# Turning blocks of rows every four steps, and a longer planned time for the addition with maximum

## The chip, the cores and the metric

The kernel runs on one core of one Trainium2 chip. The metric is the device time of one execution in microseconds (us); of several runs the median counts. The core has a matrix engine (TensorE, PE in the profile, with its weight loads as PEld), a vector engine (VectorE, DVE), an activation engine (ScalarE, ACT), a general engine (GpSimd, POOL), and a sync engine (SyncE, SP) that here only issues transfers. Each engine and each queue works through its own instructions in the order in which they were written.

## The reference

Two attention branches on the same input are mixed by a gate per row (x is 2048 rows of 512, 32 heads of 16).

```python
def _A_ref(x, wqkv, wo):          # sliding window: 8 keys, two rows apart
    ...
    idx = pos[:, None] - off[None, :]
    kg = k[:, :, idx_c, :] ; vg = v[:, :, idx_c, :]
    logits = einsum("bhsd,bhswd->bhsw", q, kg) * scale     # masked where idx < 0
    o = einsum("bhsw,bhswd->bhsd", softmax(logits), vg)
    return o.transpose(...).reshape(B, S, D) @ wo
def _B_ref(x, wq, wk, wv, wo):    # full attention, one key and value head for 32 query heads
    ...
    p = softmax(einsum("bhqd,bkd->bhqk", q, k) * scale)
    return einsum("bhqk,bkd->bhqd", p, v).transpose(...).reshape(B, S, D) @ wo
g = sigmoid((x * gate_w).sum(-1))
return g * a + (1 - g) * b
```

## The kernel before

The whole schedule is written out by one Python program, with its own clocks for PE, ACT, DVE and POOL (`clk`, `pool`). These clocks decide the order in which instructions are written, no more; on the chip semaphores decide when they run.

**First phase.** Projections of x. Their matmuls fill half of PE's rows each, and two halves side by side make a slot.

**The main loop** has 512 steps: 32 units of branch B (a block of 512 query rows by four heads), each over 16 blocks of 128 keys. In a step PE makes two pairs of score matmuls into banks `pe` (L582), ACT takes two exponentials (L584), and PE weights the values of the step before into `po` (L592). Branch B also needs the maximum of each row's scores ahead of a unit. It comes from extra score matmuls, 2048 tiles over the whole kernel, in three ways:

- a pair into both halves of bank `pm` (L393, from `fill_pair`), whose maximum DVE takes in one instruction (L422): at most one in a step;
- a single into bank `ps` (L393, from `fill_one`), reduced by L433: in the steps where `singles` allows it;
- halves (L491): from one matmul against a difference of keys ACT takes the absolute value (L520), and from one against their sum DVE adds it and takes the maximum in one instruction, with a short read of the accumulator behind it (L537, in `fill_sum`). This is done in the first phase and in the two **out phases**. Two L491 make two tiles, and each lies beside a half of the product that the phase is there for.

**The out phases** (`out_phase`) interrupt the main loop, at step 272 for rows 0 to 7 of each block of 16 and at step 416 for rows 8 to 11; they multiply the finished rows by the output weights (L889, 24 slots a row). The last four rows are done by `spread` inside the steps, from about step 481 on (L943, two or three pairs a step), once the maxima have all been taken. `fill_sum` writes a sum's matmul when the plan says that its bank (`ps` or `po`) is free, that is when the planned DVE clock has passed the sum before; `T_TTR = 0.66` us is what the plan counts for that.

**Branch A** is computed on POOL alongside (L656 to L716), in two halves of the rows, `hf` 0 and 1; `done` holds what POOL's plan has finished. A finished block of rows has to be turned before the out phase: `blocks_out` transposes a 128x256 piece on DVE (L778) into a buffer `raw` or `own`, a transfer writes it to `td` in memory (L783), and eight transfers bring it back (L791). All nine stand in SP's queue, which also loads queries (`qst<-qd`, L362 and L363) and half of the maxima (`qst<-ml`, L570). For each half there is one buffer of each kind; the four pieces queued when `hf` 1 ends (rows 8 to 11, second half of columns) all use `own`, so the transposition of one has to wait until the write of the one before has read it. `block_some(s)` runs at the end of every step and writes one transposition when its time has come.

Of the kernel before, what the change touches and what calls it, by code (L numbers as in the profile page):

```python
# [50 lines left out]
T_R, T_LAT, T_EXP, T_RED2, T_RED1, T_W, T_TTR = 0.23, 0.20, 0.92, 1.14, 0.61, 1.21, 0.66  # L51
# [30 lines left out]
def gated_mix_kernel(ctx, tc, xt, wa, wk, wq, wo_a, wo_b, out):  # L82
# [38 lines left out]
    clk = {"pe": 0.0, "act": 0.0, "dve": 0.0}  # L121

    def after(eng, ready, dur):
        clk[eng] = max(clk[eng], ready) + dur
        return clk[eng]
# [246 lines left out]
    free = {"m2": 0.0, "m1": 0.0, "e0": 0.0, "e1": 0.0, "po": 0.0}  # L372
    tasks, shifted, pm = [], set(), []
    hooks, pool, done = [], 0.0, set()
# [4 lines left out]
    def unit_tile(v):  # L379
        for x in (v, v + 1):  # L380
            if x < NU and x not in left:
                mx[x] = wp.tile([P, 2, 2, 4, 4], F32, name="mx", bufs=3)
                if pe:
                    nc.gpsimd.memset(mx[x], -FMAX)
                    charge(250)
                else:
                    nc.scalar.activation(mx[x].rearrange("p b i t k -> p (b i t k)"), ident[:, 0:64], AF.Identity, scale=0.0, bias=mk[:, 6:7])
                left[x] = NF // NU
        return mx[v]
# [8 lines left out]
    def filled(v, n):  # L398
        left[v] -= n
        if not left[v]:  # L400
            ms = wp.tile([P, 2, 2, 8], F32, name="ms")
            m = mx.pop(v).rearrange("p b i t k -> p b (i t) k")
            nc.vector.tensor_reduce(ms, m.unsqueeze(2).to_broadcast([P, 2, 2, 8, 4]), AX.X, ALU.max)
            after("dve", 0, 0.32)
            if pe:
                tasks.append((clk["pe"] + 0.5, maxima_turn, (v, ms)))
            else:
                maxima_turn(v, ms)
# [80 lines left out]
    def half_mm(dst, v, pr, t, kc, x, odd):  # L489
        b = 64 * odd  # L490
        nc.tensor.matmul(dst, qst[home(v)[0]][b:b + 62, pr, t * P:(t + 1) * P], kcd[0][b:b + 62, kc // 2, x, :], start=True, stop=True)  # L491
# [40 lines left out]
    def fill_sum(odd):  # L532
        (v, pr, t, kc), d, ready = pend[odd].pop(0)
        m = unit_tile(v)
        dst, key = ((m1, "m1"), (po, "po"))[odd]
        half_mm(dst, v, pr, t, kc, 0, odd)
        nc.vector.tensor_tensor_reduce(d[:, odd], dst, d[:, odd], 1.0, -FMAX, ALU.add, ALU.max, m[:, odd, pr, t, kc:kc + 1])  # L537
        free[key] = after("dve", max(clk["pe"] + T_R + T_LAT, ready), T_TTR) + 0.08
        filled(v, 2)

    def shift_a(v, mt):
# [33 lines left out]
    pe, pexp, exped = [], {}, {}  # L575
# [199 lines left out]
    def blocks_out(j, k):  # L775

        own = p2[0].tile([P, D // 2], F32, name="raw", tag=("raw", "own")[k if j < NJ - 4 else 0], bufs=1)
        nc.vector.transpose(own, oa[k][:, j, :])  # L778
        after("dve", clk["pe"], 0.45)
        tasks.append((clk["dve"] + 0.3, blocks_away, (j, k, own)))  # L780
# [13 lines left out]
    block_queue, turned_in, block_at = [], [], [0]  # L794

    def block_some(s):

        for hf in range(2):
            if hf in done and ("blocks", hf) not in done:
                done.add(("blocks", hf))  # L800
                block_queue.extend((j, k) for j in ((0, 1, 2, 3, 4, 5, 6, 7), (8, 9, 10, 11))[hf] for k in range(2) if (hf, k) != (1, 0))
        if 8 in done and ("blocks", 2) not in done:
            done.add(("blocks", 2))
            block_queue.extend((j, 0) for j in range(8, 12))
        if block_queue and s >= block_at[0]:
            blocks_out(*block_queue.pop(0))
            block_at[0] = s + (1 if 1 in done else 4)

    def blocks_both(j):
        blocks_out(j, 0)  # L810
# [29 lines left out]
    def stream(seq, mm, done, pooled, meet=None):  # L840
# [3 lines left out]
        while min(at) < len(seq):  # L844
# [4 lines left out]
            if halves or 1 in wants:  # L849
                for b in range(2):  # L850
                    if sum_ready(b):
                        lone[b] = lambda b=b: fill_sum(b)
                    elif diff_ready(b):
                        lone[b] = lambda b=b: fill_diff(b)
                        break
            elif fillable() and free["m1"] <= clk["pe"] - just():
                lone[half[0][4] if half else 0] = lambda: fill_one(m1, "m1")
            elif pooled and fillable() and free["po"] <= clk["pe"] - just():
                lone[half[0][4] if half else 0] = lambda: fill_one(po, "po")
# [17 lines left out]
    def out_phase(js, n, whole_unit):  # L877
# [34 lines left out]
        while groups or any(pend):  # L912
            for b in range(2):
                if sum_ready(b):
                    fill_sum(b)
                elif diff_ready(b):
                    fill_diff(b)
            clk["pe"] += T_R
# [351 lines left out]
    for s in range(NS + 1):  # L1270
# [65 lines left out]
        run_tasks()  # L1336
        run_pool()
        block_some(s)
    while later_rows:
        clk["pe"] = max(clk["pe"], spread_at[0])  # L1340
# [77 lines left out]
```

## Time and profile before

| what | value |
|---|---|
| runs shown | 1451.13, 1451.15, 1453.5 us; median 1451.15 |
| profiled execution | 1452.75 us, its span 1450.9 us |
| PE, DVE, ACT, POOL busy | 99%, 82%, 88%, 70% of the span |
| transfers | 65 GB/s over the span |
| granted TensorE clock | 0.998 |

The span is the time from the first to the last instruction; the profiled execution's own time is 1.85 us more. In the profile's rows a timeline entry is start, duration, engine, line, operation, result and operands; a bracket gives the idle time before it and what ended it.

### The profile page before, as it was taken

The page shows a single profiled execution, that of the slowest core. Times are in us where ns is not written, and L with a number is a line of the kernel's source. Part 1 is how long each engine was busy: PE and PEld are TensorE (multiplying, and loading weights), DVE is VectorE, ACT ScalarE, POOL GpSimd, SP SyncE. Part 2 cuts the span into 40 slices and gives each one's busy share as a digit, 9 for nine tenths or more (in the row PEclk, how much of TensorE's full clock was granted, in tenths as well). Part 3 has the DMA queues.
Part 4 walks back from the last instruction along what each step waited for, and adds up shares of the span by engine and source line. Part 5 has one row for each costly group of instructions (what it writes and reads, how often), then busy time and mean ns, then how long its engine had stood idle before and what let it go on. Part 6 is the DMA issues. An engine that isn't in the chain of part 4 may idle for free.

```text
span 1450.9 us, 29246 instructions
## 1 busy us (share of the span) xinstructions
PE 1440.6 (99%) x10524; PEld 672.2 (46%) x10524; DVE 1193.9 (82%) x1885; ACT 1280.9 (88%) x1608; POOL 1019.7 (70%) x1796
## 2 busy tenths in 40 slices
PE   9999999999999999999999999999999999999998
PEld 6977777433333333333333475333333336333343
DVE  8978889688888888888888898888888888888712
ACT  6659888999999999999999888999999888999986
POOL 7952989869898888888988987988888615111121
PEclk9999999999999999999999999999999999999999
DMA  7753433222021120212422200211211111000110
GB/s 238 221 157 103 125 104 98 66 55 87 14 84 42 46 90 13 72 42 75 113 72 64 75 31 31 90 54 42 72 43 42 27 26 35 9 2 2 30 30 30
DMA packets 107457, 96.12 MB, mean 66 GB/s; under 512 B 84976, under 2 KB 89120, under 8 KB 103088
## 3 DMA queue, kind: packets, MB, share of 16 engines
q1 hardware_dynamic: 100224, 55.04, 14.0%
q0 software_dynamic: 6368, 37.90, 7.7%
q8 instruction: 83, 1.36, 0.4%
q10 hardware_dynamic: 720, 1.31, 0.3%
q14 instruction: 62, 0.51, 0.1%
HBM read 63.18 MB, written 30.49 MB: 65 GB/s over the span
## 4 chain that ended last, share of the span: by engine, by line
PE 94%; POOL 2%; DVE 2%; DMA 1%; ACT 0%; issue 0%; SPq 0%; ACTq 0%; DVEq 0%
PE po L592 33%; PE pe L582 23%; PE pe L1217 12%; PE pm L393 8%; PE ps L393 6%; PE pe L889 4%; PE pm L491 3%; PE ps L491 2%; PE po L491 1%; PE pm L943 1%; POOL oa L716 1%; POOL av L713 1%; PE pe L227 1%; DMA wqr<-wq 0%; DVE pexp L537 0%
## 5 line engine op out<-in xcount | busy, mean ns | idle before, releaser
L584 ACT ACTIVATE pexp<-pe 128x1024 f32<-128x1024 f32 x1022 | 987.0, 1022 | 85.7 <-PE pe L582 81.5
L422 DVE TENSOR_REDUCE mx<-pm 128x2 f32<-128x1024 f32 x501 | 612.4, 1222 | 136.0 <-PE pm L393 131.7
L592 PE MATMUL po<-pexp,vst 128*32 128x512 f32 x4096 | 546.3, 605 | 0.0
L582 PE MATMUL pe<-qst,kst 64*128 64x512 f32 x1916 | 444.9, 452 | 0.6 <-ACT pexp L584 0.6
L582 PEld LDWEIGHTS pe<-qst,kst 64*128 64x128 f32 x1916 | 180.9, 183 | 474.1 <-ACT pexp L584 467.8
L433 DVE TENSOR_REDUCE mx<-ps 128x1 f32<-128x512 f32 x403 | 274.1, 680 | 3.7 <-PE ps L393 3.7
L393 PE MATMUL pm<-kst,qst 62*128 62x512 f32 x967 | 197.0, 398 | 3.2 <-DVE mx L422 3.2
L656 POOL TENSOR_TENSOR pr<-aext 128x256 f32<-128x256 f32 x256 | 182.1, 738 | 3.0 <-DMA aext<-ad 2.7
L716 POOL TENSOR_TENSOR oa<-oa,av 128x256 f32<-128x256 f32 x224 | 163.9, 732 | 15.5
L592 PEld LDWEIGHTS po<-pexp,vst 128*32 128x32 f32 x4096 | 80.8, 108 | 165.5 <-issue 156.1
L393 PE MATMUL ps<-kst,qst 62*128 62x512 f32 x395 | 156.2, 396 | 0.2 <-DVE mx L537 0.2
L713 POOL TENSOR_TENSOR av<-aext,lg 128x256 f32<-128x256 f32 x224 | 139.2, 622 | 12.9
L520 ACT ACTIVATE dd<-pm 128x512 f32<-128x512 f32 x180 | 101.4, 606 | 16.4 <-PE pm L491 11.2
L1217 PE MATMUL pe<-wah,xl 64*128 64x512 f32 x376 | 109.8, 393 | 0.0
L1217 PE MATMUL pe<-wal,xh 64*128 64x512 f32 x376 | 108.3, 394 | 0.0
L1217 PE MATMUL pe<-wah,xh 64*128 64x512 f32 x376 | 107.2, 395 | 0.4 <-DVE stage L324 0.3
L393 PEld LDWEIGHTS pm<-kst,qst 62*128 62x128 f32 x967 | 94.5, 187 | 7.2 <-DVE mx L422 5.0
L520 ACT ACTIVATE pexp<-pm 128x512 f32<-128x512 f32 x128 | 72.1, 599 | 15.7 <-PE pm L491 7.2
L662 POOL TENSOR_TENSOR tr<-pr 128x512 f32<-128x512 f32 x64 | 81.7, 1277 | 4.2
L662 POOL TENSOR_TENSOR tr<-tr 128x256 f32<-128x256 f32 (+1 forms) x128 | 72.5, 566 | 8.6
L393 PEld LDWEIGHTS ps<-kst,qst 62*128 62x128 f32 x395 | 73.9, 187 | 4.8 <-issue 1.2
L537 DVE CUSTOM_DVE_ANT_0 dd<-po,dd 128x512 f32<-128x512 f32 x90 | 62.1, 690 | 12.4 <-PE po L491 6.7
(222 smaller groups left out, 1942.7 us busy)
## 6 DMA issues: line engine op xcount, KB each, us to landing
aext<-ad POOLq DMA_DIRECT2D x32, 1056.0 KB, 5.6
qst<-qd SPq DMA_DIRECT2D x60, 128.0 KB
ad<-stage SPq DMA_DIRECT2D x32, 240.0 KB
qd<-qhi SPq DMA_DIRECT2D x16, 256.0 KB
qd<-qlo SPq DMA_DIRECT2D x16, 256.0 KB
td<-raw SPq DMA_DIRECT2D x32, 128.0 KB
oa<-td SPq DMA_DIRECT2D x256, 16.0 KB
xraw<-xt SPq DMA_DIRECT2D x15, 256.0 KB
```

Source lines behind the costliest of these rows:

```text
L393: nc.tensor.matmul(dst, qst[home(v)[0]][b:b + 62, pr, t * P:(t + 1) * P], kst[b:b + 62, kc * 512:(kc + 1) * 512], start=True, stop=True)
L422: nc.vector.tensor_reduce(m[:, :, pr, t, kc], dst, AX.X, ALU.max)
L433: nc.vector.tensor_reduce(m[:, odd, pr, t, kc:kc + 1], dst, AX.X, ALU.max)
L520: nc.scalar.activation(d[:, odd], m2[:, odd, :], AF.Abs)
L582: nc.tensor.matmul(bank[:, odd, :], kst[b:b + 64, kt * P:(kt + 1) * P], qst[home(u)[0]][b:b + 64, pr, :], start=True, stop=True)
L584: nc.scalar.activation(e, bank, AF.Exp, scale=SCALE)
L592: nc.tensor.matmul(po[32 * i:32 * i + 32, :], vst[:, kt, :], pexp[s, i // 2][:, i % 2, :], start=(kt == 0), stop=(kt == NJ - 1))
L656: nc.gpsimd.tensor_mul(pr[:, k], q, e[:, o:o + NH, AC:2 * AC])
L662: nc.gpsimd.tensor_add(nx, cur[:, :, 0:n], cur[:, :, n:2 * n])
L713: nc.gpsimd.tensor_mul(av, e[:, o:o + NH, 2 * AC:].rearrange("p j (h d) -> p j h d", d=DH), lg[:, w].unsqueeze(3).to_broadcast([P, NH, AG, ...
L716: nc.gpsimd.tensor_add(ao, ao, av)
L1217: nc.tensor.matmul(front[2 if x == last else x % 2][0][:, b, :], l[h], r[h], start=(i == 0), stop=(i == 3 * C - 1))
```

## The change

```diff
@@ fill_sum
-        free[key] = after("dve", max(clk["pe"] + T_R + T_LAT, ready), T_TTR) + 0.08
+        free[key] = after("dve", max(clk["pe"] + T_R + T_LAT, ready), 0.70 if pe else T_TTR) + 0.08
@@ block_some
         for hf in range(2):
             if hf in done and ("blocks", hf) not in done:
                 done.add(("blocks", hf))
+                block_at[0] = s + 2
                 block_queue.extend(...)
...
-            block_at[0] = s + (1 if 1 in done else 4)
+            block_at[0] = s + 4
```

The added line makes every line number behind it one larger. `pe` is empty in the first phase, so there 0.66 stays. Before, the blocks that follow the first half of branch A already stood four steps apart; those that follow the second half stood one step apart. Now all stand four apart, and the first of a half comes two steps after that half's end.

The counts of what PE does change in one kind of work only: 256 halves (L491) inside the out phases become 232 (168 to 156 in the first, 88 to 76 in the second), and their 24 tiles are made by 13 more matmuls into `pm` and 11 more into `ps`. The sum of matmuls is the same. Up to the first block of rows nothing moves.

**DVE where branch A ends.** First before: the transpositions (`raw<-oa`, the program's name for either buffer) stand one step apart (at the ends of steps 393 to 396), with a pair's and mostly a single's maximum between.

```order
L422 TENSOR_REDUCE mx<-pm 128x2
L778 STREAM_TRANSPOSE raw<-oa_3729 128x256
L422 TENSOR_REDUCE mx<-pm 128x2
L433 TENSOR_REDUCE mx<-ps 128x1
L778 STREAM_TRANSPOSE raw<-oa_3729 128x256
L422 TENSOR_REDUCE mx<-pm 128x2
L433 TENSOR_REDUCE mx<-ps 128x1
L778 STREAM_TRANSPOSE raw<-oa_3729 128x256
```

DVE at the same place now (ends of steps 398 and 402, then 406 and 410):

```order
L778 STREAM_TRANSPOSE raw<-oa_3729 128x256
L422 TENSOR_REDUCE mx<-pm 128x2
L433 TENSOR_REDUCE mx<-ps 128x1
L606 STREAM_TRANSPOSE tt<-po 128x512
L422 TENSOR_REDUCE mx<-pm 128x2
L433 TENSOR_REDUCE mx<-ps 128x1
L613 RECIPROCAL rl<-tt 128x16
L422 TENSOR_REDUCE mx<-pm 128x2 x2
L433 TENSOR_REDUCE mx<-ps 128x1
L778 STREAM_TRANSPOSE raw<-oa_3729 128x256
```

Four steps' maxima now stand between two transpositions. SP's queue there before:

```order
L783 DMA td<-raw 128x256 x2
L791 DMA oa_3729<-td 32x4x32 x8
L783 DMA td<-raw 128x256
L791 DMA oa_3729<-td 32x4x32 x8
L783 DMA td<-raw 128x256
L791 DMA oa_3729<-td 32x4x32 x8
L362 DMA qst_81<-qd 32x1x1024
```

SP's queue there now:

```order
L362 DMA qst_81<-qd 32x1x1024
L363 DMA qst_81<-qd 16x1024
L362 DMA qst_81<-qd 32x1x1024
L363 DMA qst_81<-qd 16x1024
L783 DMA td<-raw 128x256
L570 DMA qst_77<-ml 2x8x32 x4
L791 DMA oa_3729<-td 32x4x32 x8
L783 DMA td<-raw 128x256
```

The load of a unit's queries now goes ahead of the first write to `td`, and four transfers of maxima stand behind it.

**PE at the first out phase's start.** Before:

```order
L889 MATMUL pe_85<-wol_3733,own_10067 128x512
L889 MATMUL pe_85<-woh_3732,own_10068 128x512 x4
L491 MATMUL pm<-q_76,qst_81 128x512
L889 MATMUL pe_85<-woh_3732,own_10068 128x512
L491 MATMUL pm<-q_76,qst_81 128x512
L889 MATMUL pe_85<-woh_3732,own_10068 128x512
L889 MATMUL pe_85<-woh_3730,turned_10071 128x512
```

PE there now (the out product is L890):

```order
L393 MATMUL ps<-kst,qst_81 128x512
L890 MATMUL pe_85<-wol_3733,own_10075 128x512 x5
L890 MATMUL pe_85<-woh_3732,own_10076 128x512 x4
L393 MATMUL pm<-kst,qst_81 128x512 x2
L890 MATMUL pe_85<-woh_3732,own_10076 128x512 x4
L890 MATMUL pe_85<-woh_3730,turned_10079 128x512 x8
L890 MATMUL pe_85<-wol_3731,turned_10079 128x512 x4
L491 MATMUL pm<-q_76,qst_82 128x512
```

The halves start later, and one single and one pair are made in the phase in place of some of them.

**PE where the maxima end and the last rows begin.** Before:

```order
L393 MATMUL pm<-kst,qst_82 128x512
L582 MATMUL pe_86<-qst_81,kst 128x512 x2
L592 MATMUL po<-pexp,vst 32x512 x4
L582 MATMUL pe_85<-qst_81,kst 128x512 x2
L943 MATMUL pm<-woh_3730,turned_15910 128x512 x6
```

PE there now:

```order
L393 MATMUL pm<-kst,qst_82 128x512 x2
L582 MATMUL pe_86<-qst_81,kst 128x512 x2
L592 MATMUL po<-pexp,vst 32x512 x4
L582 MATMUL pe_85<-qst_81,kst 128x512 x2
L393 MATMUL pm<-kst,qst_82 128x512 x2
L582 MATMUL pe_86<-qst_81,kst 128x512 x2
L592 MATMUL po<-pexp,vst 32x512 x4
L582 MATMUL pe_85<-qst_81,kst 128x512 x2
L944 MATMUL pm<-woh_3730,turned_15928 128x512 x6
```

Two more steps take a pair of maxima, the last rows' products begin two steps later, and six later steps (493 to 498) then hold three pairs of those products where they held two.

## The prediction

> **What bounds the kernel.** I read the page's head and chain first, then single steps in the timeline, then the steps that are longer than their kind.
>
> ```profile
> span 1450.9 us, 29246 instructions
> PE 1440.6 (99%) x10524; PEld 672.2 (46%) x10524; DVE 1193.9 (82%) x1885; ACT 1280.9 (88%) x1608; POOL 1019.7 (70%) x1796
> PE 94%; POOL 2%; DVE 2%; DMA 1%; ACT 0%; issue 0%; SPq 0%; ACTq 0%; DVEq 0%
> ...
> 707.79 0.50 PE L582 MATMUL pe<-qst,kst 64*128 64x512 f32 x2
> 709.69 0.49 PE L582 MATMUL pe<-qst,kst 64*128 64x512 f32 x2
> 710.25 0.40 PE L393 MATMUL ps<-kst,qst 62*128 62x512 f32 x1
> 711.81 0.50 PE L582 MATMUL pe<-qst,kst 64*128 64x512 f32 x2
> ...
> 728.16 0.50 PE L582 MATMUL pe<-qst,kst 64*128 64x512 f32 x2
> 730.29 0.49 PE L582 MATMUL pe<-qst,kst 64*128 64x512 f32 x2
> ```
>
> PE is busy for 99% and carries 94% of the chain, so time is won where PE's row is shorter or where it waits. The first L582 of a step marks its start. A step with a pair of maxima takes 1.90 us (707.79 to 709.69), one that also holds a single 2.12 (709.69 to 711.81): a single costs 0.22 and makes one tile. The step at 728.16 holds a single and no pair, and takes 2.13 all the same: a pair put there is free.
>
> The long steps stand together where branch A ends:
>
> ```profile
> 1150.27 0.73 POOL L716 TENSOR_TENSOR oa<-oa,av 128x256 f32<-128x256 f32 x1
> 1151.03 0.45 DVE L778 STREAM_TRANSPOSE raw<-oa 128x256 f32<-128x256 f32 x1 [1.73 <-POOL oa L716]
> 1151.33 0.51 PE L582 MATMUL pe<-qst,kst 64*128 64x512 f32 x2
> 1152.64 0.50 PE L393 MATMUL pm<-kst,qst 62*128 62x512 f32 x2 [0.81 <-DVE mx L422]
> 1155.58 0.45 DVE L778 STREAM_TRANSPOSE raw<-oa 128x256 f32<-128x256 f32 x1
> 1158.03 0.38 SPq L783 DMA_DIRECT2D td<-raw  x1
> 1158.84 0.49 PE L582 MATMUL pe<-qst,kst 64*128 64x512 f32 x2
> 1159.89 0.45 DVE L778 STREAM_TRANSPOSE raw<-oa 128x256 f32<-128x256 f32 x1 [2.16 <-DMA td<-raw]
> 1161.50 0.50 PE L393 MATMUL pm<-kst,qst 62*128 62x512 f32 x2 [2.17 <-DVE mx L422]
> 1163.82 0.79 PE L582 MATMUL pe<-qst,kst 64*128 64x512 f32 x2
> 1171.60 0.49 PE L582 MATMUL pe<-qst,kst 64*128 64x512 f32 x2
> ...
> 1158.00:1162.00 4.00, 1.83 (x14) 0.64 (x8) 2.04 (x4) 2.46 (x3) 0.00 (x0) 1.00 0.30 63
> 1162.00:1167.00 5.00, 5.00 (x27) 1.54 (x24) 3.66 (x5) 2.96 (x3) 3.07 (x7) 0.66 0.28 56
> ```
>
> The first transposition stood 1.73 in DVE until POOL's last sum of branch A, the fourth 2.16 until the third's write, issued 2.4 after it, had left the buffer. The maxima queue behind them on DVE, and PE waits for the bank: 0.81 and 2.17. (The windows' columns are PE, PEld, DVE, ACT and POOL busy, then the granted clock.) PE is busy for 1.83 of the 4 us around the second wait, and in the next 5 us the clock is 0.66, a loss of 5 x 0.34 = 1.7.
>
> **A: spacing and the two steps of delay.** From 1151.33 to 1171.60 are seven steps, 20.27 us, one of them without a single: 6 x 2.12 + 1.90 = 14.62 is their kind's price, 5.65 too much. Now transpositions are four steps apart, 8.5 us; from the third's end (1156.03) to its buffer's release (1159.89) were 3.9, with eight transfers ahead in SP's queue. The first comes five steps later, 10.6 us, past POOL's end even if PE runs ahead by what the out phase saves. Each still takes its 0.45 of DVE, in a step whose maxima use 1.91 of 2.12; the blocks after the first half stand like that already, and no long step is quoted from there. Nothing left is the likeliest, nothing gained the other end, and I take -5.6.
>
> ```profile
> 1167.43 0.54 SPq L362 DMA_DIRECT2D qst<-qd  x1
> 1169.37 0.58 SPq L363 DMA_DIRECT2D qst<-qd  x1
> ```
>
> What moves with a block are one transposition, one write and eight readings. On SP the first write now stands behind four loads of queries (2.5 us from the first's start to the last's end), which makes 3.9 + 2.5 = 6.4, under 8.5; the four loads run earlier than before, so nobody waits for them. The rows are wanted at step 416, six steps (12.7 us) after the last transposition, and row 11 three rows later still. The blocks of rows 0 to 7 and the first halves of rows 8 to 11 move by two steps: at nothing, since step 272 and step 416 lie 20 and 115 steps behind.
>
> **B and C: the two out phases.**
>
> ```profile
> 833.52 0.39 PE L491 MATMUL po<-q,qst 62*128 62x512 f32 x1
> 834.22 0.40 PE L491 MATMUL ps<-q,qst 62*128 62x512 f32 x1
> ...
> 834.06 0.69 DVE L537 CUSTOM_DVE_ANT_0 pexp<-po,pexp 128x512 f32<-128x512 f32 x1 [0.23 <-PE po L491]
> 834.68 0.08 DVE L537 DVE_READ_ACCUMULATOR2_ANT mx<- 128x1 f32 x1
> 834.76 0.69 DVE L537 CUSTOM_DVE_ANT_0 pexp<-ps,pexp 128x512 f32<-128x512 f32 x1
> ...
> 823.91:894.32 70.41, 54.27 (x168) 28.84 (x168) 0.00 (x0) 1.00 0.13 45
> 1201.07:1238.09 37.02, 36.83 (x293) 25.42 (x293) 32.73 (x97) 31.75 (x54) 22.18 (x38) 1.00 0.08 26
> ...
> PEld po L491 <- DVE mx L537: 5.6, 25, 0.4
> PEld ps L491 <- DVE mx L537: 4.7, 22, 0.4
> ```
>
> Three slots lie between 833.52 and 834.22: 0.233 each. DVE's sums follow each other in 0.70 (834.06 to 834.76), where the plan counted 0.66. The first phase's window holds 168 halves of maxima (the row is of their tile alone) beside 8 rows x 48 halves of product: 276 slots, 64.3 us. With the step's own 1.67 (1.90 less the pair) and a pair and two singles (0.46), 66.4 of 70.41 are accounted for; 4.0 are lost. The plan's debt is 84 sums x 0.04 = 3.4, and the loader's waits for L537 are there (5.6 + 4.7 in this phase, partly under running matmuls). In the second phase 88 + 192 halves are 140 slots, 32.6, and 1.8 for the rest: 2.6 lost, debt 44 x 0.04 = 1.8.
>
> With 0.70 the plan writes a sum when its bank is really free. Twelve halves fewer are six slots: -1.40 in each phase. The first gains a pair and a single (+0.35), the second a pair (+0.23). Of the lost time I take three quarters of the debt as gone, -2.6 and -1.3, since a phase's start, its seams and DVE's few other instructions stay; the ends are 0 and all that is lost. B = -3.65, C = -2.47. ACT loses twelve absolute values, DVE twelve sums: both have more room.
>
> **D: the tiles that come back to the main loop.** By the rows of the order, ten more steps hold a single (the eleventh is in B): 10 x 0.22 = +2.2. The steps that gain a pair had none: free, as at 728.16. In the tail:
>
> ```profile
> 1372.50 0.50 PE L582 MATMUL pe<-qst,kst 64*128 64x512 f32 x2
> 1374.85 0.51 PE L582 MATMUL pe<-qst,kst 64*128 64x512 f32 x2
> ...
> 1401.02 0.51 PE L582 MATMUL pe<-qst,kst 64*128 64x512 f32 x2
> 1403.14 0.50 PE L582 MATMUL pe<-qst,kst 64*128 64x512 f32 x2
> ...
> 1238.09:1372.50 134.41, 134.41 (x951) 48.57 (x947) 114.57 (x135) 123.39 (x129) 13.25 (x30) 1.00 0.04 9
> ```
>
> Two steps with three pairs of product (2.35) become steps with a pair of maxima (1.90), -0.9; six with two pairs (2.12) become ones with three, +1.4. D = +2.7, from 0 (were all those steps bound by something else) to +3.1. Nine of the ten singles fall between the second out phase and the tail, where DVE is busy for 114.57 of 134.41: 9 x 0.68 more makes 120.7 of 136.4, 88%, so they are covered.
>
> **The sum.** -5.6 - 3.65 - 2.47 + 2.7 = -9.0. The profiled execution took 1452.75 (span 1450.9 and 1.85 around it): 1443.75, I say 1443.8. That execution is 1.6 above the median of 1451.15 (the other runs: 1451.13 and 1453.5), about the 1.7 that its clock lost after the stall. If the median's runs didn't pay this, they gain 7.3 and come to 1443.85: the same.
>
> **A rule on the clock.** The row is the 0.66 after a stretch that was under half busy. The Trainium skill says in "TensorE: Matmul & The Clock Gate", section "What's actually happening", that the clock halves after an idle window of about 3.4 us, and that the window runs freely, so the same work falls differently into it from run to run. By that rule the clock's 1.7 belongs to some executions and not to others, and A is 3.9 and the sum -7.3 in those without it; the trace agrees that the clock drops after the wait, and one profile cannot show the rest.
>
> **The rivals.**
> - *The clock's loss is in every run.* For it: the wait is there whatever the run. Then the median falls by all 9.0: 1442.2. Against: the runs' spread of 1.6 to 2.4.
> - *The out phases keep their waits*, because in them DVE was busy for 32.73 of 37.02 and its sums simply move closer to the end. Then only slots go: -5.6 - 1.05 - 1.17 + 2.7 = -5.1, 1447.6. Against: the loss (4.0, 2.6) is close to the debt (3.4, 1.8) in both.
> - *The waits at branch A's end come back in the new places.* Then A is nothing and the sum -3.4: 1449.4 against the profiled execution, 1447.8 against the median. Against: 6.4 is under 8.5.
> - *Slower: each of the four transpositions waits for the write before it*, since SP's order now has loads and maxima between. Price by the step at 1158.84 (4.98, to 1163.82): 2.86 a wait and 1.7 of clock behind it, four times 4.6 = 18.2, against the 5.6 that go, with B, C and D -3.4: +9.2, 1460. It decides once a wait costs over 9.0 / 4 = 2.3. For it: SP is one queue. Against: a write would have to stay 8.5 us behind, 2.1 more than worked out above.
>
> **How the numbers follow.** Forecast 0.50, clock in every run 0.18, out phases unchanged 0.16, waits come back 0.10, slower 0.04, other things 0.02. The range reaches up to the second rival and the third's lower value, 1448.0, and down to all that B and C lost being gone (another -2.7, 1441.1) and half of the clock's 1.6 beside it, 1440.3; beyond lie the fourth rival, half of the third, and both low ends in full. A measurement of this kernel tells 0.2%, 2.9 us, from no change: faster is below 1448.25. That gives 0.87 faster, 0.08 the same, 0.05 slower.
>
> **What would show it.** Right: no step from the last sum of branch A to step 416 above 2.4 us, no clock below 0.95 there, no wait of L778 for `td` before the tail; windows of the out phases near 66.8 and 34.6; steps with a single still 2.12. Wrong: L778 waiting for `td<-raw` after branch A, loader waits for L537 of the old size, or steps behind the second out phase above 2.2, DVE then being the bound.

## The result: 1444.2 against 1452.2 us

The median fell from 1452.22 us (1451.13 to 1453.5) to 1444.19 (1443.88 to 1444.74), a ratio of 0.9946 with a 95% interval of 0.9933 to 0.9958. Taken again later, it was 1444.4, ratio 0.9943 (0.993 to 0.9955). The forecast was 1443.8. The profiled execution took 1444.01 (span 1442.2), 8.74 less than the one before. One of the runs below, the profiled one of delay_only, took 4497.31 us at a recorded clock of 1.000, its weighting matmuls (L592) 1734 ns each where they else take 605; why is not known, and it is left out of that kernel's median.

The profile after, in the order of the prediction's: head and chain of waits, the timeline at branch A's end, stretches (columns PE, PEld, DVE, ACT, POOL, clock), and the loader's waits in the first out phase (sum, number, mean).

```profile
span 1442.2 us, 29203 instructions
PE 1435.9 (100%) x10524; PEld 674.7 (47%) x10524; DVE 1199.8 (83%) x1878; ACT 1274.5 (88%) x1596; POOL 1019.4 (71%) x1796
PE 99%; DVE 1%; ACT 0%; issue 0%; POOL 0%; DVEq 0%; ACTq 0%; POOLq 0%
...
1152.06 0.50 PE L582 MATMUL pe<-qst,kst 64*128 64x512 f32 x2
1153.28 0.74 POOL L716 TENSOR_TENSOR oa<-oa,av 128x256 f32<-128x256 f32 x1
1156.68 0.40 DVE L778 STREAM_TRANSPOSE raw<-oa 128x256 f32<-128x256 f32 x1
1157.70 1.22 SPq L783 DMA_DIRECT2D td<-raw  x1
1164.87 0.43 DVE L778 STREAM_TRANSPOSE raw<-oa 128x256 f32<-128x256 f32 x1
1166.61 0.50 PE L582 MATMUL pe<-qst,kst 64*128 64x512 f32 x2
1169.40 0.38 SPq L783 DMA_DIRECT2D td<-raw  x1
1173.66 0.43 DVE L778 STREAM_TRANSPOSE raw<-oa 128x256 f32<-128x256 f32 x1
...
1152.06:1166.61 14.55, 14.53 (x107) 5.33 (x103) 13.21 (x19) 13.51 (x15) 5.77 (x13) 1.00 0.13 38
824.18:891.92 67.74, 67.60 (x565) 50.00 (x561) 60.56 (x172) 55.56 (x97) 60.19 (x97) 1.00 0.12 43
1192.44:1227.16 34.72, 34.58 (x287) 24.72 (x283) 30.64 (x87) 27.66 (x48) 21.09 (x34) 1.00 0.08 27
1227.16:1363.00 135.84, 135.82 (x955) 48.62 (x955) 118.68 (x141) 124.03 (x129) 14.22 (x34) 1.00 0.04 8
...
PEld po L491 <- DVE mx L537: 4.4, 22, 0.4
PEld ps L491 <- DVE mx L537: 3.1, 16, 0.4
```

PE now carries 99% of the chain instead of 94%. None of the four transpositions has a bracket any more (the fourth starts at 1182.18): POOL's last sum ends at 1154.02, well ahead of 1156.68, and each write leaves its buffer before the next transposition. The same seven steps take 14.55 us at clock 1.00 where they took 20.27 with 5 us at 0.66. Only the first transposition still falls into them; the other three stand in steps 403, 407 and 411, which take 2.12 to 2.13. Both out phases are shorter, yet the loader still waits there for L537: 7.5 us in 38 waits, where it was 10.3 in 47.

From the starts of the steps in the traces, this is where the 8.64 us of span went, and what the experiments' profiles show in the same places. Numbers are differences to before in us, columns are steps of the main loop: 272 and 416 with the two out phases, 273 to 299 with the first halves of rows 8 to 11, 395 to 401 with the end of branch A, 417 to 480 up to the last rows. Halves are L491 in the two out phases.

| kernel | halves | step 272 | 273 to 299 | 395 to 401 | 416 | 417 to 480 | all else | span |
|---|---|---|---|---|---|---|---|---|
| before, us | 168 + 88 | 70.41 | 57.53 | 20.27 | 37.02 | 134.40 | | 1450.9 |
| after | 156 + 76 | -2.68 | -1.29 | -5.70 | -2.30 | +1.54 | +1.79 | -8.64 |
| space_only | 164 + 80 | -0.20 | -1.16 | -5.41 | -1.06 | +1.03 | +0.07 | -6.73 |
| four_only | 168 + 88 | +0.11 | +0.26 | -4.11 | +0.17 | -0.03 | +0.18 | -3.42 |
| two_buf | 168 + 88 | -0.01 | -0.03 | -4.13 | +0.11 | +0.05 | -0.15 | -4.15 |
| delay_look | 164 + 80 | -0.12 | -1.07 | +2.34 | -0.69 | +1.02 | +0.71 | +2.20 |
| ttr_only | 164 + 76 | -1.45 | +0.05 | -3.59 | -1.97 | +1.38 | +1.24 | -4.34 |
| all70 | 164 + 84 | -1.60 | -0.97 | -5.58 | -1.34 | +0.71 | +1.83 | -6.95 |
| on_time | 156 + 80 | -3.83 | -1.30 | -5.71 | +0.88 | +1.51 | +1.72 | -6.73 |
| ttr072 | 160 + 64 | +2.45 | +1.05 | -5.20 | -0.76 | +2.39 | +1.48 | +1.42 |
| ttr074 | 152 + 80 | -2.78 | +1.49 | -5.58 | +1.10 | +1.79 | +2.13 | -1.85 |
| ttr078 | 144 + 72 | -0.16 | +1.65 | -5.37 | -2.28 | +2.32 | +3.49 | -0.35 |

The places don't hold the same work in each kernel. By the counts of L393 in the traces, after has two singles fewer than before in steps 273 to 299 and one fewer in 395 to 401, at 0.22 each; space_only and delay_look have one fewer in each. These singles stand in other steps. In most of the other kernels it differs by one or two as well.

### The profile page after: what moved, and what is told of

It is laid out like the page before. It is cut to its first block, busy times and chain, and to the rows that moved or that the text cites. A ratio compares the mean times of both kernels' runs of the same rounds, so it can differ in the third digit from the quotient of the medians.

```text
span 1442.2 us, 29203 instructions
## 1 busy us (share of the span) xinstructions
PE 1435.9 (100%) x10524; PEld 674.7 (47%) x10524; DVE 1199.8 (83%) x1878; ACT 1274.5 (88%) x1596; POOL 1019.4 (71%) x1796
## 4 chain that ended last, share of the span: by engine, by line
PE 99%; DVE 1%; ACT 0%; issue 0%; POOL 0%; DVEq 0%; ACTq 0%; POOLq 0%
PE po L592 35%; PE pe L582 24%; PE pe L1218 12%; PE pm L393 8%; PE ps L393 6%; PE pe L890 5%; PE pm L491 3%; PE ps L491 2%; PE pm L944 1%; PE po L491 1%; PE pe L227 1%; PE po L193 0%; PE po L393 0%; PE pm L1218 0%; PE po L1043 0%; PE ps L1043 0%
## 5 line engine op out<-in xcount | busy, mean ns | idle before, releaser
L422 DVE TENSOR_REDUCE mx<-pm 128x2 f32<-128x1024 f32 x508 | 621.0, 1223 | 131.0 <-PE pm L393 125.6
L592 PE MATMUL po<-pexp,vst 128*32 128x512 f32 x4096 | 545.5, 605 | 0.0
L433 DVE TENSOR_REDUCE mx<-ps 128x1 f32<-128x512 f32 x414 | 281.6, 680 | 3.3 <-PE ps L393 3.3
L393 PE MATMUL pm<-kst,qst 62*128 62x512 f32 x980 | 201.3, 396 | 0.1
L393 PE MATMUL ps<-kst,qst 62*128 62x512 f32 x406 | 160.0, 394 | 0.0
L592 PEld LDWEIGHTS po<-pexp,vst 128*32 128x32 f32 x4096 | 80.5, 108 | 166.4 <-issue 157.0
L393 PEld LDWEIGHTS pm<-kst,qst 62*128 62x128 f32 x980 | 96.9, 186 | 2.8 <-DVE mx L422 0.6
L520 ACT ACTIVATE pexp<-pm 128x512 f32<-128x512 f32 x116 | 65.0, 600 | 15.3 <-PE pm L491 8.8
L393 PEld LDWEIGHTS ps<-kst,qst 62*128 62x128 f32 x406 | 75.8, 187 | 3.7 <-issue 1.2
L537 DVE CUSTOM_DVE_ANT_0 dd<-po,dd 128x512 f32<-128x512 f32 x90 | 62.1, 690 | 12.5 <-PE po L491 7.3
```

The source lines that it names most:

```text
L422: nc.vector.tensor_reduce(m[:, :, pr, t, kc], dst, AX.X, ALU.max)
L433: nc.vector.tensor_reduce(m[:, odd, pr, t, kc:kc + 1], dst, AX.X, ALU.max)
L520: nc.scalar.activation(d[:, odd], m2[:, odd, :], AF.Abs)
L592: nc.tensor.matmul(po[32 * i:32 * i + 32, :], vst[:, kt, :], pexp[s, i // 2][:, i % 2, :], start=(kt == 0), stop=(kt == NJ - 1))
```

## The experiments

Theory: branch A's end is won by taking away the wait for the buffer and the clock's loss behind it (spacing) and the wait for POOL (delay); the out phases are won by the sums being written on time.

**space_only**: the changed kernel with the old price.

```diff
-        free[key] = after(..., 0.70 if pe else T_TTR) + 0.08
+        free[key] = after(..., T_TTR) + 0.08
```

> The delay and the four steps alone; the plan counts 0.66 for a sum as before. Theory (spacing wins where branch A ends, the planned time wins in the out phases): the seven long steps lose their 5.7 us, the waits behind step 285 their 1.3, three more singles cost 0.7; the out phases hold 164 and 80 halves and, for their slots, still lose 4.0 and 2.6 us. 1445 to 1446.5. Rival (the out phases lose by the number of their sums, whatever the plan counts): their loss shrinks here too, by a fifth, and the time is below 1445.

Measured 1446.46, ratio 0.9962 (0.9949 to 0.9976). Spacing and delay carry the 5.4 at branch A's end, as expected. The table also shows what the expectation of this run had and the prediction had not: with the old price too there are 12 halves fewer, and steps 273 to 299 gain 1.16.

**ttr_only**: the kernel before with the new price alone.

```diff
-        free[key] = after(..., T_TTR) + 0.08
+        free[key] = after(..., 0.70 if pe else T_TTR) + 0.08
```

> 0.70 for a sum alone; blocks stand one step apart as before. Theory: the steps where branch A ends keep 5 to 6 us of waiting and a clock below 1.0; the out phases (164 and 76 halves) lose 2.4 and 1.5 in place of 4.0 and 2.6 and have two and six slots fewer; nine more singles cost 2.0 and the tail 0.5. Together -1 to -2.5: 1449.5 to 1451. Rival (the planned time moves the whole order and so the blocks too): the waits at branch A's end change by more than 2 us, either way.

Measured 1448.01, ratio 0.9973 (0.9963 to 0.9984): a miss, too good by 1.5 to 3; the rival was right. The price alone took 3.59 from branch A's end, where it changes no spacing. The transpositions came one step later, and the wait for the buffer fell where PE had work, into a step (399) that holds no pair of maxima:

```profile
1152.11 0.45 DVE L778 STREAM_TRANSPOSE raw<-oa 128x256 f32<-128x256 f32 x1 [1.77 <-POOL oa L716]
1160.92 0.45 DVE L778 STREAM_TRANSPOSE raw<-oa 128x256 f32<-128x256 f32 x1 [1.53 <-DMA td<-raw]
1162.53 0.18 PEld L393 LDWEIGHTS pm<-kst,qst 62*128 62x128 f32 x2 [0.32 <-DVE mx L422]
1158.00:1162.00 4.00, 4.00 (x31) 1.28 (x27) 2.40 (x6) 3.63 (x5) 1.89 (x5) 1.00 0.30 65
```

DVE waited 1.53 for the buffer, but PE was busy for all of 4.00 us at clock 1.00; the step behind it took 2.75, 0.6 over its kind, where before lost 2.86 and the clock. So the parts don't add: alone they bring 4.4 (price) and 5.9 (space_only), together 8.0.

**two_buf**: before's order unchanged, but the four late pieces alternate between the two buffers, so that no transposition needs the write just ahead of it.

```diff
-  tag=("raw", "own")[k if j < NJ - 4 else 0]
+  tag=("raw", "own")[j % 2 if k and 8 <= j < NJ - 4 else k if j < NJ - 4 else 0]
```

> The kernel before, in the same order, only that the four late pieces use the two buffers in turn, so that a transposition waits for the write of the piece two before. Theory (the fourth's wait is for its buffer, and the clock falls because of it): no wait of a transposition for td there, clock 1.0, the steps from 1158.84 lose 2.9 + 1.1, the first's wait for POOL (1.2) stays: -3.9 to -4.4, 1447.8 to 1448.4. Rival (transpositions crowd DVE itself, the buffer matters little): under -1, above 1451.

Measured 1448.63, ratio 0.9977 (0.9968 to 0.9986), a little less gained than expected.

```profile
1150.80 0.45 DVE L778 STREAM_TRANSPOSE raw<-oa 128x256 f32<-128x256 f32 x1 [1.74 <-POOL oa L716]
1152.41 0.50 PE L393 MATMUL pm<-kst,qst 62*128 62x512 f32 x2 [0.83 <-DVE mx L422]
1156.98 0.43 DVE L778 STREAM_TRANSPOSE raw<-oa 128x256 f32<-128x256 f32 x1
1151.06:1167.20 16.14, 15.31 (x108) 5.44 (x104) 15.67 (x23) 13.83 (x15) 3.91 (x9) 1.00 0.26 56
```

With no instruction moved, 4.13 us vanish from those seven steps and nothing elsewhere exceeds 0.22. The clock stays at 1.00, though PE still waits 0.83 for POOL. That shows the cause: 2.2 of wait for the buffer and 1.7 of clock behind it, as the prediction worked out.

**four_only** and **delay_only**: spacing without delay, and delay without spacing, both with the old price.

```diff
 four_only
-            block_at[0] = s + (1 if 1 in done else 4)
+            block_at[0] = s + 4
 delay_only
+                block_at[0] = s + 2
...
             block_at[0] = s + (1 if 1 in done else 4)
```

> Four steps between transpositions, no delay, 0.66: the out phases hold 168 and 88 halves as before, so only the end of branch A differs. Theory: the fourth's wait for its buffer goes with what hangs on it (4.1, as with two buffers), the first's wait for POOL and PE's 1.2 there stay: 1448 to 1448.8. Rival (spacing takes more than the buffer's wait away, since the transpositions also crowd DVE): 1447 or less.

Measured 1448.84, ratio 0.9976 (0.9967 to 0.9986). It gains 4.11 at the same place as two_buf and nothing elsewhere. Delay adds 1.3 there (5.41 in space_only); 0.22 of it is the single that stands elsewhere, so 1.1 is its own.

> Two steps of delay, but one step apart and 0.66. Theory: the first's wait for POOL and PE's 0.8 behind it go, the fourth's wait for its buffer (PE 2.2, and the clock) stays; slots as in the run with the spacing alone, against which this is 4 to 4.5 slower: about 1449.5 to 1450.5. Rival (the delay is what frees the fourth as well, since POOL's end no longer holds DVE back): equal to the run with the spacing alone within 1.

Measured 1455.14 (median of eight runs, without the one of 4497.31), slower: ratio 1.0019 (1.0009 to 1.0029), a miss of 4.6 to 5.6. The profile comes from a further run of the same kernel, **delay_look**:

> The kernel of the run with the delay alone (3.2 us slower than before), for a profile of an ordinary execution. Theory: two and more of the four transpositions, one step apart, wait for the write of the one before; the seven steps there take 8 us or more over their kind, and the clock falls below 0.8 behind them. Rival: the four stand as before and the loss is in the out phases (164 and 80 halves) or in the steps behind them.

It took 1454.85, and the seven steps 8.2 over their kind, as expected:

```profile
1157.07 2.72 SPq L570 DMA_DIRECT2D qst<-ml  x4
1158.19 0.45 DVE L778 STREAM_TRANSPOSE raw<-oa 128x256 f32<-128x256 f32 x1 [0.72 <-DMA td<-raw]
1159.89 4.03 SPq L791 DMA_DIRECT2D oa<-td  x8
1164.02 0.38 SPq L783 DMA_DIRECT2D td<-raw  x1
1165.85 0.45 DVE L778 STREAM_TRANSPOSE raw<-oa 128x256 f32<-128x256 f32 x1 [5.51 <-DMA td<-raw]
1167.46 0.79 PE L393 MATMUL pm<-kst,qst 62*128 62x512 f32 x2 [5.15 <-DVE mx L422]
1165.00:1170.00 5.00, 2.54 (x13) 1.03 (x13) 3.48 (x6) 1.02 (x1) 0.00 (x0) 0.53 0.48 135
```

The first transposition comes three steps later than before (step 397), and there four loads of maxima (2.72) and eight readings (4.03) stand in SP's queue between the second transposition (ended 1158.64) and its write (1164.02). The next transposition waits 5.51, PE 5.15, and the clock falls to 0.53. This is the mechanism of the prediction's slower rival, at a spacing of one step instead of four, and with one long wait instead of four (the others are 0.72 and 0.67). Delay alone costs 2.34 in these steps; behind a spacing of four it gains 1.1.

**all70**: the new price in the first phase as well.

```diff
-        free[key] = after(..., 0.70 if pe else T_TTR) + 0.08
+        free[key] = after(..., 0.70) + 0.08
```

> The changed kernel with 0.70 for a sum in the first phase too. Theory (a truer plan lets PE wait less): the first phase holds 8 halves fewer (four slots, 0.9) and loses 1 to 2 us less in its 180 sums; the out phases hold 164 and 84; three singles more. Net -2 to -1 against the changed kernel's 1444.2: 1442 to 1443.2. Rival (in the first phase PE is not held by DVE's sums, the tiles only move to the main loop): 1444.2 to 1446.

Measured 1446.34, ratio 0.9959 (0.9945 to 0.9973), 2 us worse than after and 0.3 above the rival's range. The rival's mechanism was right: the first phase is only 0.7 shorter than in after, less than its four slots, the steps from there to 272 are 1.7 longer, and the out phases got 8 + 8 halves back.

**ttr072, ttr074, ttr078**: other prices in place of 0.70, everything else as after.

> 0.72 in place of 0.70: 160 and 64 halves, one single fewer in the main loop, three more singles and three more pairs within the phases. Theory of lumps: a few waits fewer or more, the time within 1 of the changed kernel. Rival (time rises with the plan's price from 0.70 on, as 0.78 did by 8): 1446 or more.

> 0.74: 152 and 80 halves, the same count of singles as the changed kernel, and the first late block of rows at step 285 as before. Theory of lumps: waits of pm's matmul for ScalarE begin to show in the first phase, +0 to +3: 1444 to 1447. Rival (time rises steadily from 0.70 to 0.78): 1447 to 1449.

> The changed kernel with 0.78 in place of 0.70 (144 and 72 halves in the out phases, nine more singles in the main loop). Theory (what the phases lose is the plan's debt): the loss falls to under 1 us in each phase, six and two slots fewer save 1.9, nine singles cost 2.0 and the tail 0.5: 1442.5 to 1443.8. Rival (the loss has causes that the plan's price doesn't touch): losses stay at 2.4 and 1.5, the time is 1444.5 to 1446.

Measured 1455.22 (ratio 1.0017, 1.0008 to 1.0026), 1450.83 (0.999, 0.9981 to 0.9999) and 1452.51 (1.0, 0.9992 to 1.0009): the theories missed all three, and so did the rivals of ttr074 and ttr078. The rival of ttr072 has the right range, but not the right reason: the time doesn't rise with the price, 0.72 is the slowest. The two phases together hold fewer halves than after in ttr072 and ttr078 and as many in ttr074, but another wait comes in. These are the loader's waits of the first out phase for ACT, of after, ttr072 and ttr078:

```profile
PEld pm L491 <- ACT pexp L520: 1.1, 6, 0.2
```

```profile
PEld pm L491 <- ACT pexp L520: 7.9, 30, 0.5
```

```profile
PEld pm L491 <- ACT pexp L520: 10.8, 38, 0.6
```

Step 272 pays for it in ttr072 (+5.1 against after) and ttr078 (+2.5); in ttr074 the second phase does (+3.4). The bank of the differences (`pm`), which ACT reads, is then the one not free. The second cost is a moved order at the blocks behind step 272, in ttr072 thus:

```profile
927.38 0.43 DVE L778 STREAM_TRANSPOSE raw<-oa 128x256 f32<-128x256 f32 x1
927.84 5.21 SPq L570 DMA_DIRECT2D qst<-ml  x8
933.30 0.60 SPq L362 DMA_DIRECT2D qst<-qd  x1
935.91 0.37 SPq L783 DMA_DIRECT2D td<-raw  x1
937.93 0.45 DVE L778 STREAM_TRANSPOSE raw<-oa 128x256 f32<-128x256 f32 x1 [2.18 <-DMA td<-raw]
939.55 0.50 PE L393 MATMUL pm<-kst,qst 62*128 62x512 f32 x2 [1.63 <-DVE mx L422]
```

Here four steps were not enough: eight loads of maxima and four of queries (the first is shown) held the write back until 8.1 us after its transposition.

**on_time**: a sum's matmul is written only when the plan has its bank free, without the 0.1 us ahead that is allowed in the loop (`just()` is -0.1 there).

```diff
-        ... free[("m1", "po")[odd]] <= clk["pe"] - just() and ...
+        ... free[("m1", "po")[odd]] <= clk["pe"] - max(0.0, just()) and ...
```

> The changed kernel, but in the out phases a sum's matmul is no longer written up to 0.1 us ahead of its bank's planned release (156 and 80 halves; two singles fewer in the main loop). Theory (a matmul that waits, however briefly, costs a lump of about 0.235: its own slot 0.13 longer and the next 0.105): of six such waits for sums in the first phase two to five go, -0.5 to -1.2, singles -0.4: 1442.5 to 1443.5. Rival (the loss is the plan's debt on DVE and not the number of waits): 1444 to 1445.

Measured 1445.68, ratio 0.9952 (0.994 to 0.9965), above both ranges and 1.3 worse than after_again. Stretches of the two phases, and the loader's wait for ACT in the second:

```profile
824.51:891.09 66.58, 66.44 (x563) 48.65 (x559) 60.37 (x172) 55.50 (x97) 60.23 (x97) 1.00 0.13 47
1191.60:1229.51 37.91, 36.91 (x292) 24.70 (x288) 31.11 (x90) 30.30 (x50) 22.23 (x38) 1.00 0.07 25
PEld pm L491 <- ACT pexp L520: 5.9, 21, 0.5
```

The first phase gained 1.15 more, within what was expected of it, though hardly for the reason given: the loader still waits 36 times for L537 there (38 in after), but never longer than 0.2 us (0.4 in after). The second lost 3.2: four halves more, and 5.9 of waits for ACT (1.3 in after).

**after_again**: the changed kernel beside these.

> The changed kernel again, on the chip of the next three: 1444.2 within 1, and a spread of its runs of 1 or less, since no wait at branch A's end lets the clock fall; the kernel before spreads over 2 and more.

Measured 1444.4 (1444.1 to 1444.73). No kernel tried was faster.

## Why the prediction was right, and where not

**A (-5.6): right, -5.70**, or -5.5 without the single that left these steps. Spacing takes 4.1 (four_only, and two_buf by another way), delay 1.1 behind it; the last 0.3 came with the price, and why is open. The cost of DVE's 0.45 was hidden as said: the seven steps and the three with the other transpositions stand at their kind's price.

**The clock: settled, as the prediction split it.** Over the 61 runs of before that stand beside the experiments, sorted by granted clock:

| granted clock | before: runs, mean us | after: runs, mean us |
|---|---|---|
| 1.000 | 22, 1451.36 | 11, 1444.36 |
| 0.999 | 22, 1452.75 | none |
| 0.998 | 14, 1452.90 | none |
| 0.997 | 3, 1454.45 | none |

About a third of the runs of before (22 of 61) show no loss of clock, and these stand 7.0 above after (7.3 said); those at 0.998, like the profiled one, stand 8.5 above (9.0 said). The rival of a loss in every run is out; the median's gain of 8.0 lies between because most runs pay. What failed is the remark that the profiled execution is 1.6 above the median: that was a median of three runs, and with 19 to 21 it was 1452.4 to 1452.7, within 0.4 of the profiled one's. By the rule that the Trainium skill gives in "TensorE: Matmul & The Clock Gate", section "What's actually happening", the window runs freely, so that the same stall can fall into it in one run and not in another; the runs agree: one kernel, one order, clocks from 0.997 to 1.000, and ttr072 with its new stall again spreads (1454.05 at 1.000, 1457.92 at 0.996). The idle window of about 3.4 us that the prediction quotes with this rule is not what the trace shows: the clock fell after a wait of 2.17, with PE busy for 1.83 of the 4 us around it.

**B (-3.65): right in sign, a third too large; -2.68.** The slots (-1.40) and the pair and single (+0.35) were as counted. The mis-sized term is the lost time: three quarters of the debt, 2.6, were taken as gone, and 67.74 less 270 slots (62.9), 1.67 and 0.81 leaves 2.4 of the 4.0 lost, so 1.6 went. One wait shows why a shorter debt isn't time won in proportion (matmuls, then weight loads, of before):

```profile
869.15 0.40 PE L491 MATMUL pm<-q,qst 62*128 62x512 f32 x1
869.53 0.50 PE L491 MATMUL po<-q,qst 62*128 62x512 f32 x1
869.53 0.73 PE L889 MATMUL pe<-woh,own 64*128 64x512 f32 x3
870.10 0.39 PE L491 MATMUL pm<-q,qst 62*128 62x512 f32 x1
...
869.52 0.18 PEld L491 LDWEIGHTS po<-q,qst 62*128 62x128 f32 x1 [0.40 <-DVE mx L537]
869.53 0.52 PEld L889 LDWEIGHTS pe<-woh,own 64*128 64x128 f32 x4
```

The late slot starts 0.38 behind the one before it, and the next slot again late: 0.57 lie between 869.53 and 870.10, two slots of 0.233 and 0.10, since its weights began to load only behind the load that had waited. So this wait cost a quarter of a microsecond, of which nearly half falls behind the late slot. Summed over the phase, slots that hold a half start late by 2.3 before and 1.0 after; the slots of two products, by 1.0 and 0.8; the other 0.7 of the 4.0 lay in the step's own matmuls, and 0.6 of it stayed. Plan and chip still part by small amounts (38 waits are left), and on_time, which gives the plan no lead, brought the phase's loss down to some 1.2. That the lumps are the whole reason is argued, not shown.

**C (-2.47): right, -2.30**, by the same split (1.1 of the lost time where 1.3 was taken).

**The blocks after the first half, "at nothing": wrong, -1.29**, of which 0.44 is the two singles that left these steps and 0.85 time won. Moving these blocks by two steps was thought to be without weight. Before and after, at the first piece of rows 8 to 11:

```profile
922.28 0.73 POOL L716 TENSOR_TENSOR oa<-oa,av 128x256 f32<-128x256 f32 x1
923.05 0.44 DVE L778 STREAM_TRANSPOSE raw<-oa 128x256 f32<-128x256 f32 x1 [1.04 <-POOL oa L716]
924.65 0.50 PE L393 MATMUL pm<-kst,qst 62*128 62x512 f32 x2 [0.21 <-DVE mx L422]
```

```profile
922.81 0.73 POOL L716 TENSOR_TENSOR oa<-oa,av 128x256 f32<-128x256 f32 x1
923.85 0.40 DVE L778 STREAM_TRANSPOSE raw<-oa 128x256 f32<-128x256 f32 x1
924.10 5.34 SPq L570 DMA_DIRECT2D qst<-ml  x8
930.03 0.34 SPq L783 DMA_DIRECT2D td<-raw  x1
931.83 0.45 DVE L778 STREAM_TRANSPOSE raw<-oa 128x256 f32<-128x256 f32 x1
```

A transposition waited for POOL there too, 1.04, and after has no such wait. The prediction had taken the absence of a very long step for the absence of a wait. The added line doesn't do this by itself: these four pieces are queued on `8 in done`, which sets no `block_at`. The delay of the earlier blocks moved the plan (four_only, without it, gains nothing here, space_only 1.16), and the plan then queued them at the end of step 287 instead of 285. With the same line ttr074 starts them at 285 and waits 0.87 for POOL, and ttr078 starts them at 287 and waits 1.54. So this gain is partly luck.

**D (+2.7): right, +2.7.** The steps up to 480 outside the places above took 2.9 more, for 13 singles more: the ten of the prediction and the three that left 273 to 299 and 395 to 401. That is 0.22 each, as said, and 0.7 of the 2.9 belongs to those places. DVE is busy for 118.68 of 135.84 us, 87%, and covers them (88% said). The tail took 0.8 where 0.5 was said; the first phase, which the change leaves alone, came out 0.3 shorter.

**The reason given for fewer halves** was wrong in half of it: all 24 were put to the price. space_only loses 12 of them with the old price, four_only none, so 12 come with the delay, which shifts what the plan finds ready at each out phase. The price alone loses 16 (ttr_only). The total didn't suffer, since space_only's own gain at the out phases is small (0.20 and 1.06).

**The margin of 8.5 us** held, but 6.4 was too small for the worst place: at 924 the write goes out 5.8 us after its transposition ended. With the 1.86 from the third's write (1158.03) to its release (1159.89) in before, that makes 7.6, an estimate, and the next transposition comes after just that (931.83). ttr072 reorders SP a little and it fails. The slower rival was thus nearer in the neighbouring kernels than its 4%; delay_look shows its kind of cost, a wait that reaches PE plus clock, once and not four times.

The errors (B's +1.0, C's +0.2 and A's +0.1 against the blocks' -0.85) nearly cancel, and that the sum came within half a microsecond is to that extent luck.

What stays open: whether a truer price for ACT's absolute value, set together with a higher one for DVE, would free the out phases of both waits. No run tries it.

## What to carry to other kernels

A wait of another engine that reaches PE costs its stall, and in some runs the clock lost behind it as well; the runs sorted by granted clock show how many of them pay. When a hand-over has one buffer, space its users by what the transfer queue can hold ahead of the release at the worst place, not by the usual row; moving the first user alone made it worse. A planner's price above the measured period doesn't help while the other prices are not true as well: above 0.70 the waits moved from DVE's bank to ACT's.

## What the runs showed of the hardware

- In the wait shown, the loads behind a weight load that waits start late as well, and so the slot after the late slot is late too: 0.10 us after a delay of 0.15 (869.53 in before). At 851.55 in after it is 0.10 after 0.13.
- Issuing has a price on SP that depends on the transfer: eight loads of maxima took 5.21 to 5.34 us in the lines shown, eight readings of the turned rows 4.03, and a write that stands behind them waits for all.
- In the profiled runs PE waits of 0.83 (two_buf) and 1.63 (ttr072) left the clock at 1.00 in the stretch around them, a wait of 2.17 (before) brought 0.66, one of 5.15 (delay_look) brought 0.53. Runs of one kernel differ in this, as the table of clocks shows.
